# The high part of p on VectorE instead of ScalarE in the loop's last steps

## The chip, the cores and the metric

The kernel runs on one core of a Trainium2 chip. The metric is device time in microseconds (us). A core has five engines, each with its own queue of instructions in a fixed order: TensorE (PE, matrix products), VectorE (DVE), ScalarE (ACT), GpSimd (POOL) and SyncE (SP, which here issues all DMAs). An engine starts an instruction when it is at the head of its queue and its semaphores have come.

## The reference

```python
def _A_ref(x, wqkv, wo):                 # H = 32 heads of 20, window W = 256
    q, k, v = ...                        # x @ wqkv
    scores = einsum("bhqd,bhkd->bhqk", q, k) * Dh ** -0.5
    mask = (idx[:, None] - idx[None, :] >= 0) & (idx[:, None] - idx[None, :] < W)
    p = softmax(where(mask, scores, -1e9))
    o = einsum("bhqk,bhkd->bhqd", p, v)
    return o... @ wo
def _B_ref(x, w1, b1, w2, b2):
    r = relu(x @ w1 + b1)
    return (r * r) @ w2 + b2

xn = layernorm(x)                        # x: 1 x 2048 x 640, f32
return x + _A_ref(xn) * silu(_B_ref(xn))
```

## The kernel before

Products are made in f16 with each operand split in a high and a low part (high = the value rounded to f16, low = the rest), so that a product is three matmuls: high x high, high x low, low x high. The same holds for the softmax weights p: `ph` is p in f16, `pl` is p - ph in f16, and both are multiplied with the values (which have their own two parts in one tile).

After a first stage (layernorm, transposes, values, first queries and keys) a loop of 269 steps runs over 16 pairs of heads (`NP`) times 16 blocks of 128 rows (`NT`), 256 blocks in all, as a software pipeline. In step s:

- the scores of block s (`scores`, L585) and their row maxima (`maxima`, L596, VectorE), as long as s < 256
- `scores_t` (L634, TensorE): the transposed scores of block s-10, into the one PSUM tile `stps`
- `exps` of block s-10: the exponential on ScalarE (L639, from stps into one of three `p32` tiles, `p` in the profile), then two masks on GpSimd (L640, L642)
- `low` of block s-12 (L653, VectorE): pl = p32 - ph. It is the last reader of that p32 tile
- a first share of filler work on TensorE (queries and keys, MLP, output products), then evacuations of filler results (`flush`: `ysb` L936, `sq` L909 on VectorE) and one piece of weight preparation (`tick`: in these steps wo, L1004 high part and L1005 low part, both VectorE)
- `high` of block s-11 (L647): ph from p32
- the rest of the filler share
- in every second step `values` (L667, TensorE) of blocks s-14 and s-13, which read ph and pl; every fourth block ends a group, followed by `normed` (ACT L674 `osb`, DVE L678 `rs`, POOL L680 and L683) and `halves_high`/`halves_low` (ACT L694, DVE L698 `onp`), whose results go to DRAM

All engines run in the order in which the program calls them (`manual_schedule`); there is no scheduler. `state[2]` holds the step number. The steps from 256 to 268 have no scores and no maxima; they finish blocks 246 to 255. Their row maxima still go from a copy `mrow` (L617) by DMA into `qs`, which scores_t reads. Tiles in rotation: three of p32, six of ph, five of pl, one of stps.

Behind the loop the output products (`wops`, L731) run on TensorE, with L1023 and L1024 on VectorE and a Silu on ScalarE (L1038).

Of the kernel before, what the change touches and what calls it, by code (L numbers as in the profile page):

```python
# [11 lines left out]
AF = mybir.ActivationFunctionType  # L12
# [8 lines left out]
NT = S // P  # L21
KC = D // P
NP = H // 2
# [35 lines left out]
def attn_mlp_kernel(ctx: ExitStack, tc, x, wqkv, wo, w1, b1, w2, b2, out):  # L59
    nc = tc.nc  # L60
# [583 lines left out]

    def high(p, kb, p32, n):
        ph = at4.tile([P, 2, 3 * P], F16, tag="ph", name="ph")
        nc.scalar.activation(ph[:, :, :n], p32[:, :, :n], AF.Copy)  # L647
        phs[p, kb] = (ph, p32, n)

    def low(p, kb):  # L650
# [52 lines left out]
    state = [0.0, 0.0, 0]  # L703
# [378 lines left out]
    with tc.manual_schedule(engines={E_.PE, E_.Activation, E_.DVE, E_.Pool, E_.SP}):  # L1082
# [5 lines left out]
        for s in range(steps):  # L1088
# [51 lines left out]
            if c:  # L1140
                high(*c, *exs.pop(c))
# [44 lines left out]
```

## Time and profile before

| | us |
|---|---|
| median of 3 runs | 814.17 (813.47 to 814.29) |
| the profiled execution | 814.96 |
| its span, first to last instruction | 813.2 |
| steps from the first without scores to the last pl | about 715.5 to 742.2 |
| first and last `ph` of the eleven that the change moves | 717.68, 740.04 |

A row of the timeline gives start and duration in us, engine, line, operation, what it writes and reads, and in brackets how long the engine had been idle before it and what it waited for. A row of a window gives busy time of PE, weight loads, DVE, ACT and POOL in that stretch, each with a count of instructions. In rows grouped by line stand busy time, the mean in ns, and idle time before it with its cause.

### The profile page before, as it was taken

What the parts mean: (1) busy time and instruction counts of PE and PEld (TensorE: products, weight loads), DVE (VectorE), ACT (ScalarE), POOL (GpSimd) and SP (SyncE); (2) the same over time, 40 slices, a digit from 0 to 9 for tenths busy, and PEclk for the clock granted to TensorE, in tenths of its full rate; (3) what the DMA queues carried; (4) which work ended last, traced back from release to release, by engine and by line L of the source; (5) the groups of instructions that cost most, each with busy time, mean ns of one, the idle gap of its engine ahead of it and who ended that gap; (6) DMA issues with size and microseconds to landing.
All of it is one profiled execution on the core that took longest, in us unless ns stands there. A gap on an engine that the chain in (4) does not pass through costs nothing.

```text
span 813.2 us, 25075 instructions
## 1 busy us (share of the span) xinstructions
PE 802.0 (99%) x9358; PEld 536.3 (66%) x9358; DVE 698.0 (86%) x1948; ACT 644.6 (79%) x1059; POOL 498.8 (61%) x874
## 2 busy tenths in 40 slices
PE   8999999999999999999999999999999999999998
PEld 7775563455555567777777777777777767767776
DVE  6777666798999999999999999999999999996554
ACT  5466454999899999899999999999989989987200
POOL 2000001467677789897988889888978988783000
PEclk9999999999999999999999999999999999999999
DMA  7995757774665532221222222222221362156994
GB/s 246 256 337 154 195 162 230 241 200 113 160 178 141 158 93 69 58 71 35 69 67 39 68 72 55 55 68 52 51 71 36 86 220 59 14 141 162 281 285 143
DMA packets 157137, 105.49 MB, mean 130 GB/s; under 512 B 101080, under 2 KB 131544, under 8 KB 157016
## 3 DMA queue, kind: packets, MB, share of 16 engines
q1 hardware_dynamic: 157016, 103.90, 46.3%
q8 instruction: 73, 1.20, 0.6%
q14 instruction: 48, 0.39, 0.2%
HBM read 60.43 MB, written 36.83 MB: 120 GB/s over the span
## 4 chain that ended last, share of the span: by engine, by line
PE 82%; ACT 6%; DVE 5%; DMA 3%; issue 3%; SPq 0%; DVEq 0%; ACTq 0%
PE hps L731 20%; PE yps L932 18%; PE wops L731 8%; PE ops L667 8%; PE qkps L731 7%; PE sps L585 7%; PE vps L303 6%; PE stps L634 4%; PE qkps L529 3%; ACT p L639 2%; DVE pl L653 1%; DMA raw<-in_B_w_dram 1%; DMA wvr<-in_A_wqkv_dram 1%; DVE junk L596 1%; DMA raw<-in_A_wqkv_dram 1%
## 5 line engine op out<-in xcount | busy, mean ns | idle before, releaser
L639 ACT ACTIVATE p<-stps,ebias,esc 128x768 f32<-128x768 f32 (+2 forms) x256 | 242.1, 946 | 36.4 <-PE stps L634 15.9
L653 DVE TENSOR_TENSOR pl<-p,ph 128x768 f16<-128x768 f32 (+2 forms) x256 | 250.9, 980 | 0.9 <-PE ops L667 0.8
L596 DVE CUSTOM_DVE_ANT_0 junk<-sps,mask 128x320 bf16<-128x320 f32 (+2 forms) x512 | 220.1, 466 | 27.2 <-PE sps L585 23.6
L640 POOL TENSOR_SCALAR_AFFINE_SELECT p<-p 128x256 f32<-128x256 f32 x256 | 176.3, 689 | 63.9 <-ACT p L639 61.7
L647 ACT ACTIVATE ph<-p 128x768 f16<-128x768 f32 (+2 forms) x256 | 203.0, 793 | 1.0 <-POOL p L640 0.8
L731 PE MATMUL hps<-xT,w 128*128 128x256 f16 x1440 | 190.0, 273 | 0.0
L932 PE MATMUL yps<-w,hh 128*128 128x320 f16 x1152 | 186.7, 300 | 0.0
L731 PEld LDWEIGHTS <-w 128*128 128x128 f16 x1440 | 132.4, 98 | 45.0 <-issue 25.5
L932 PEld LDWEIGHTS <-hh 128*128 128x128 f16 x1152 | 105.0, 98 | 54.9 <-issue 20.9
L731 PE MATMUL qkps<-xT,qkw 128*128 128x512 f16 x480 | 115.5, 380 | 0.0
L642 POOL TENSOR_SCALAR_AFFINE_SELECT p<-p 128x256 f32<-128x256 f32 x224 | 107.6, 480 | 0.0
L667 PE MATMUL ops<-vp,ph 128*128 128x41 f16 x1440 | 89.8, 181 | 0.0
L667 PE MATMUL ops<-vp,pl 128*128 128x41 f16 x1440 | 89.5, 180 | 0.0
L667 PEld LDWEIGHTS <-ph 128*128 128x128 f16 x1440 | 84.6, 96 | 5.2
L585 PE MATMUL sps<-ks,qs 60*64 60x320 f16 (+2 forms) x1024 | 84.5, 313 | 3.2 <-DVE mt L596 2.7
L667 PEld LDWEIGHTS <-pl 128*128 128x128 f16 x1440 | 78.9, 96 | 5.1
L634 PE MATMUL stps<-qs,ks 62*64 62x320 f16 (+4 forms) x1024 | 78.5, 290 | 1.3 <-ACT p L639 0.9
L910 POOL TENSOR_TENSOR hh<-sq,hh 128x256 f16<-128x256 f32 x96 | 66.5, 693 | 21.0 <-DVE sq L909 13.8
L603 POOL CAST mp<-mt 128x8 f16<-128x8 f32 x64 | 45.1, 705 | 54.2 <-DVE mt L596 53.8
L731 PEld LDWEIGHTS <-qkw 128*128 128x128 f16 x480 | 42.5, 98 | 53.5 <-issue 11.0
L303 PE MATMUL vps<-wv,xT 128*128 128x320 f16 x480 | 69.6, 299 | 1.3 <-DVE xT L277 0.4
L731 PE MATMUL wops<-wo,oT 128*128 128x320 f16 (+1 forms) x495 | 65.6, 295 | 0.0
(153 smaller groups left out, 993.3 us busy)
## 6 DMA issues: line engine op xcount, KB each, us to landing
raw<-in_B_w_dram SPq DMA_DIRECT2D x24, 320.0 KB
ks<-k_d SPq DMA_DIRECT2D x64, 120.0 KB
qs<-q_d SPq DMA_DIRECT2D x64, 120.0 KB
v_d<-vt SPq DMA_DIRECT2D x8, 656.0 KB
vp<-v_d SPq DMA_DIRECT2D x16, 328.0 KB
xt<-in_A_x_dram SPq DMA_DIRECT2D x16, 320.0 KB
k_d<-shm SPq DMA_DIRECT2D x20, 256.0 KB
q_d<-shm SPq DMA_DIRECT2D x20, 256.0 KB
```

The costliest lines, as they stand in the source:

```text
L303: nc.tensor.matmul(ps, xT[b][:, xp, c, t * P:(t + 1) * P], wv[wp][:, c, nh * HALF:(nh + 1) * HALF], start=n == 0, stop=n == 3 * KC - 1)
L585: nc.tensor.matmul(ps[HB * j:HB * (j + 1), :nk], qs[i][rows_, q0:q0 + HB], ks[i][rows_, k0:k0 + nk], start=True, stop=True)
L596: nc.vector.tensor_tensor_reduce(out=junk[:, :nk], in0=ps[:, :nk], in1=mk, scale=1.0 / MAX_UNIT, scalar=-3.0e38, op0=ALU.add, op1=ALU.max, ...
L634: nc.tensor.matmul(ps[HB * j:HB * (j + 1), hh, c0:c1], ks[i][rows_, kb * P + HB * j:kb * P + HB * (j + 1)], qs[i][rows_, kb * P + c0:kb * ...
L639: nc.scalar.activation(p32[:, :, :n], ps[:, :, :n], AF.Exp, scale=esc[0], bias=ebias)
L640: nc.gpsimd.affine_select(p32[:, :, 0:P], p32[:, :, 0:P], pattern=[[0, 2], [1, P]], compare_op=ALU.is_ge, fill=0.0, base=0, channel_multip ...
L642: nc.gpsimd.affine_select(p32[:, :, 2 * P:], p32[:, :, 2 * P:], pattern=[[0, 2], [-1, P]], compare_op=ALU.is_gt, fill=0.0, base=0, channel ...
L647: nc.scalar.activation(ph[:, :, :n], p32[:, :, :n], AF.Copy)
L653: nc.vector.tensor_sub(pl[:, :, :n], p32[:, :, :n], ph[:, :, :n])
L667: nc.tensor.matmul(ot[:, q % 4, hh, :], t[:, hh, (q - k) * P:(q - k + 1) * P], vp[:, k // 4, k % 4, hh, :], start=m == 1, stop=m == 2 * le ...
L731: nc.tensor.matmul(ps, a, b_, start=j == 0, stop=j == n - 1)
L932: nc.tensor.matmul(ps, hh[:, hp, tt * P:(tt + 1) * P], lin1(w2t, (2 * fc + wp) * D + nh * HALF, HALF), start=fc == 0 and j == 0, stop=fc = ...
```

## The change

In steps 256 and later, `high` makes ph on VectorE instead of ScalarE. Nothing else is edited; lines below it move down by three.

```diff
     def high(p, kb, p32, n):
         ph = at4.tile([P, 2, 3 * P], F16, tag="ph", name="ph")
-        nc.scalar.activation(ph[:, :, :n], p32[:, :, :n], AF.Copy)
+        if state[2] < NP * NT:
+            nc.scalar.activation(ph[:, :, :n], p32[:, :, :n], AF.Copy)
+        else:
+            nc.vector.tensor_copy(ph[:, :, :n], p32[:, :, :n])
         phs[p, kb] = (ph, p32, n)
```

Step 256 converts block 245 and step 266 block 255, so eleven conversions change engine. In the rows that follow, `p_15267` is the p32 tile of block 245, `p_15296` that of 246, then `p_15364`, `p_15400`, `p_15451`, `p_15484` (block 250), `p_15541` and `p_15575` (block 252).

VectorE's queue at steps 256 to 258, before:

```order
L909 TENSOR_TENSOR sq<-relu 128x256
L617 COPY mrow<-mtp 16x128
L678 RECIPROCAL rs<-osb 128x8
L653 TENSOR_TENSOR pl<-p_15267,ph 128x768
L936 SCALAR_TENSOR_TENSOR ysb<-yps,w_i,b2t 128x320
L1004 TENSOR_SCALAR wo_13868<-raw,wo_s 128x640
L1005 SCALAR_TENSOR_TENSOR wo_13868<-raw,wo_s,wo_13868 128x640
L653 TENSOR_TENSOR pl<-p_15296,ph 128x768
```

and with the change:

```order
L912 TENSOR_TENSOR sq<-relu 128x256
L650 CAST ph<-p_15267 128x768
L617 COPY mrow<-mtp 16x128
L681 RECIPROCAL rs<-osb 128x8
L656 TENSOR_TENSOR pl<-p_15267,ph 128x768
L939 SCALAR_TENSOR_TENSOR ysb<-yps,w_i,b2t 128x320
L1007 TENSOR_SCALAR wo_13868<-raw,wo_s 128x640
L1008 SCALAR_TENSOR_TENSOR wo_13868<-raw,wo_s,wo_13868 128x640
L650 CAST ph<-p_15296 128x768
L656 TENSOR_TENSOR pl<-p_15296,ph 128x768
```

The first conversion stands ahead of mrow and rs, the second directly ahead of the pl that reads it.

The same queue at steps 260 to 264, where the wo pieces end, before:

```order
L678 RECIPROCAL rs<-osb 128x8
L653 TENSOR_TENSOR pl<-p_15451,ph 128x768
L1004 TENSOR_SCALAR wo_13869<-raw,wo_s 128x640
L1005 SCALAR_TENSOR_TENSOR wo_13869<-raw,wo_s,wo_13869 128x640
L653 TENSOR_TENSOR pl<-p_15484,ph 128x768
L936 SCALAR_TENSOR_TENSOR ysb<-yps,w_i,b2t 128x320
L653 TENSOR_TENSOR pl<-p_15541,ph 128x768
L698 TENSOR_TENSOR onp<-on,onp 128x160
L653 TENSOR_TENSOR pl<-p_15575,ph 128x768
```

and with the change:

```order
L650 CAST ph<-p_15451 128x768
L681 RECIPROCAL rs<-osb 128x8
L656 TENSOR_TENSOR pl<-p_15451,ph 128x768
L1007 TENSOR_SCALAR wo_13869<-raw,wo_s 128x640
L1008 SCALAR_TENSOR_TENSOR wo_13869<-raw,wo_s,wo_13869 128x640
L650 CAST ph<-p_15484 128x768
L656 TENSOR_TENSOR pl<-p_15484,ph 128x768
L939 SCALAR_TENSOR_TENSOR ysb<-yps,w_i,b2t 128x320
L650 CAST ph<-p_15541 128x768
L656 TENSOR_TENSOR pl<-p_15541,ph 128x768
L650 CAST ph<-p_15575 128x768
L701 TENSOR_TENSOR onp<-on,onp 128x160
```

Each step gains one conversion behind its evacuation or wo piece; it waits for GpSimd's masks of its block, and the pl behind it waits for it instead of for ScalarE.

ScalarE's queue at steps 256 to 258, before:

```order
L907 ACTIVATE hh<-relu 128x256
L647 ACTIVATE ph<-p_15267 128x768
L674 ACTIVATE osb<-ops 128x328
L639 ACTIVATE p_15364<-stps,ebias,esc 128x768
L647 ACTIVATE ph<-p_15296 128x768
L639 ACTIVATE p_15400<-stps,ebias,esc 128x768
```

and with the change:

```order
L910 ACTIVATE hh<-relu 128x256
L677 ACTIVATE osb<-ops 128x328
L639 ACTIVATE p_15364<-stps,ebias,esc 128x768
L639 ACTIVATE p_15400<-stps,ebias,esc 128x768
L639 ACTIVATE p_15451<-stps,ebias,esc 128x768
```

The conversions are gone from it, so osb and the exponentials follow each other directly. The queues of TensorE, GpSimd and SyncE keep their instructions and their order.

## The prediction

> **What bounds the kernel now.** First the page's busy times and the windows by stage.
>
> ```profile
> span 813.2 us, 25075 instructions
> PE 802.0 (99%) x9358; PEld 536.3 (66%) x9358; DVE 698.0 (86%) x1948; ACT 644.6 (79%) x1059; POOL 498.8 (61%) x874
> 719.00:736.00 17.00, 16.26 (x187) 11.07 (x186) 16.48 (x23) 12.30 (x16) 13.36 (x19) 1.00 0.82 210
> 736.00:746.00 10.00, 10.00 (x137) 7.70 (x135) 5.04 (x9) 6.50 (x11) 3.13 (x5) 1.00 0.74 206
> 745.96 63.90 PE L731 MATMUL wops<-wo,oT 128*128 128x320 f16 x484
> ```
>
> (The window rows give length, then busy time of PE, weight loads, DVE, ACT and POOL, the granted clock and the DMA.) Over the whole span TensorE is the bound: 802.0 of 813.2 us. The change only touches the steps behind the last scores, so the row that decides is that of 719 to 736 us. There VectorE (DVE) is the full engine, 16.48 of 17.00 us, and ScalarE (ACT) has 4.70 us free. TensorE loses 0.74 us. Behind it, from 745.96 us, TensorE runs the output products without a hole to the end: what it loses ahead of them is added to the span in full.
>
> Next, who waits for whom between 719 and 740 us, and the rows behind it (start, duration, and in brackets the wait that came before):
>
> ```profile
> ACT p L639 <- DVE pl L653: 3.4, 4, 1.2
> PE stps L634 <- ACT p L639: 0.5, 2, 0.4
> 734.43 0.99 ACT L639 ACTIVATE p<-stps,ebias,esc 128x768 f32<-128x768 f32 x1 [0.93 <-DVE pl L653]
> 736.28 0.77 ACT L639 ACTIVATE p<-stps,ebias,esc 128x512 f32<-128x512 f32 x1
> 725.28 0.50 PE L634 MATMUL stps<-qs,ks 62*64 62x320 f16 x4 [0.20 <-DMA qs<-mrow]
> 732.81 0.33 PE L634 MATMUL stps<-qs,ks 62*64 62x320 f16 x4 [0.37 <-ACT p L639]
> 735.47 0.30 PE L634 MATMUL stps<-qs,ks 62*64 62x256 f16 x4 [0.18 <-ACT p L639]
> 737.76 0.24 PE L634 MATMUL stps<-qs,ks 62*64 62x128 f16 x4
> ```
>
> This is a ring over three engines. The exponentials of key block k write a p32 tile; there are three, so they need the one that pl of block k-3 has read. TensorE's next stps needs the one stps bank, which those exponentials read. So a late pl on VectorE delays an exponential, and that delays TensorE's queue. At 735.47 us TensorE waits 0.18 us for the exponential that began at 734.43 us, which had waited 0.93 us for pl: the ring is closed here, with no slack left. One step on, the exponential of 736.28 us ends at 737.05, 0.71 us ahead of the stps at 737.76: slack is back.
>
> **The change part by part.** Eleven conversions leave ScalarE and enter VectorE: steps 256 to 266 convert key blocks 245 to 255. Nine are 128x768, the last two 128x512 and 128x256. ScalarE is freed of 0.83 us a step, but it waits in these steps anyway. VectorE gets the conversion behind the evacuations and the wo piece of the step, right ahead of the next pl, which then waits for it. Here is VectorE's queue at the place:
>
> ```profile
> 717.48 0.62 DVE L909 TENSOR_TENSOR sq<-relu 128x256 f32<-128x256 f32 x1
> 718.02 0.20 DVE L617 COPY mrow<-mtp 16x128 f16<-16x128 f16 x1
> 718.87 0.20 DVE L678 RECIPROCAL rs<-osb 128x8 f32<-128x8 f32 x1 [0.64 <-ACT osb L674]
> 718.99 0.91 DVE L653 TENSOR_TENSOR pl<-p,ph 128x768 f16<-128x768 f32 x1
> 720.28 0.72 DVE L1004 TENSOR_SCALAR wo<-raw,wo_s 128x640 f16<-128x640 f32 x1
> 721.03 0.90 DVE L1005 SCALAR_TENSOR_TENSOR wo<-raw,wo_s,wo 128x640 f16<-128x640 f32 x1
> 721.86 1.21 DVE L653 TENSOR_TENSOR pl<-p,ph 128x768 f16<-128x768 f32 x1
> 729.12 0.54 DVE L1004 TENSOR_SCALAR wo<-raw,wo_s 128x640 f16<-128x640 f32 x1
> 733.18 1.15 DVE L653 TENSOR_TENSOR pl<-p,ph 128x768 f16<-128x768 f32 x1
> 734.72 0.94 DVE L653 TENSOR_TENSOR pl<-p,ph 128x768 f16<-128x768 f32 x1
> ```
>
> *The price c of one conversion.* The trace of before has none on VectorE. Nearest is wo's high part, also f32 to f16 from SBUF, one input tensor, 640 elements a row.
>
> ```profile
> L1004 DVE TENSOR_SCALAR wo<-raw,wo_s x5: 537/689/721, 720.3 to 731.6; 128x640 f16<-128x640 f32 x5
> L246 DVE TENSOR_SCALAR xn<-xt,mv,rstd x16: 611/612/614, 5.6 to 81.6; 128x640 f32<-128x640 f32 x16
> L653 DVE TENSOR_TENSOR pl<-p,ph 128x768 f16<-128x768 f32 x224 | 232.6, 1038 | 0.1
> 728.42 0.71 POOL L680 TENSOR_TENSOR on<-osb 128x160 f32<-128x160 f32 x1 [0.49 <-ACT osb L674]
> 729.92 0.93 POOL L640 TENSOR_SCALAR_AFFINE_SELECT p<-p 128x256 f32<-128x256 f32 x1 [0.79 <-ACT p L639]
> 724.84 1.12 POOL L642 TENSOR_SCALAR_AFFINE_SELECT p<-p 128x256 f32<-128x256 f32 x1
> 725.61 0.69 DVE L1004 TENSOR_SCALAR wo<-raw,wo_s 128x640 f16<-128x640 f32 x1
> ```
>
> The fast one of the five (0.54 us, at 729.12) fell almost wholly into a hole of GpSimd (729.13 to 729.92 us); the one at 725.61 us began under a select and took 0.69. A second per-partition operand costs about 0.07 us (0.61 of xn against 0.54), so with none the 640 elements take an estimated 0.47 us. 128 more elements add 0.11 us at that row's rate (0.54/640 each): 0.58 us free of GpSimd, and 0.15 more beside a select, 0.73. I take **c = 0.65 us**, between them, since GpSimd is busy 13.36 of 17.00 us but with holes. The ends: 0.50 (640 elements in 0.54 us, less the operand, with nothing for length) and 1.04 us, the mean of a pl, if the conversion runs like an operation of two tensors. Below nothing it can't go: it is work added to an engine that is full.
>
> The Trainium skill, "VectorE: DVE Perf Modes", section "The perf-mode tier table", gives 1227 ns for an f32 copy of 2048 elements in SBUF, twice as fast as a two-tensor operation; scaled by its rate of two elements a cycle, the estimate is 0.56 us for 768 elements, and the sum below would be 2.5 us by it.
>
> *What lies beside other work.* The first conversion, block 245, comes between sq and mrow at 718.02 us. VectorE idles 0.64 us right there, waiting for osb, and osb on ScalarE stood behind a conversion that is gone:
>
> ```profile
> 717.68 0.83 ACT L647 ACTIVATE ph<-p 128x768 f16<-128x768 f32 x1
> 718.41 0.42 ACT L674 ACTIVATE osb<-ops 128x328 f32<-128x328 f32 x1
> 717.71 0.18 PE L667 MATMUL ops<-vp,pl 128*128 128x41 f16 x1
> 717.63 0.50 SPq L1013 DMA_DIRECT2D xres<-in_A_x_dram  x1
> 718.25 1.39 SPq L711 DMA_DIRECT2D qs<-mrow  x2
> xres<-in_A_x_dram SPq DMA_DIRECT2D x1, 1280.0 KB
> ```
>
> With the values done at about 717.89 us, osb can end at 718.4 instead of 718.83. Then 718.02 + 0.65, mrow, rs (each starting some 0.08 us ahead of the end before it) let pl of block 245 begin at 718.82 instead of 718.99: c - 0.82 = -0.17 us. For this one the cover is complete; without it, it would cost c more, 0.65 us. mrow goes out about 0.6 us later on SP's queue; its landing, which TensorE waited for at 725.28 us (0.20 us), came seven microseconds after the copy, behind the load of xres (1280 KB in one issue) ahead of it on that queue. So I cost it at nothing; uncovered, it would cost TensorE 0.6 us at that place, not in addition, since the ring delays the later stps by more.
>
> *What lies on the path.* Between pl of block 245 and pl of block 250 (733.18 us) VectorE gets five conversions in a full queue. Three stand right ahead of their pl, which must wait for the result: c + 0.03 each (wo's low part begins 0.03 us behind the high part: 720.28 + 0.72 to 721.03). Two have onp or rs between, where the next starts some 0.08 us before the end: c - 0.08 each. Sum: -0.17 + 3 x 0.68 + 2 x 0.57 = **3.0 us** (6c - 0.9 in general). So pl of block 250 ends at 737.3 instead of 734.33 us, its exponential starts at 737.4 and ends at 738.4, and stps of step 264 starts 3.0 us later, at 738.5 instead of 735.47. ScalarE does not bind here: one exponential of 0.99 us a step is left to it.
>
> Behind that the wo pieces are over. pl of block 251 ends 3.7 us later, at 739.4 (735.66 before, plus c + 0.03), the exponential of block 254 at 740.2, and TensorE reaches its stps at 737.76 + 3.0 = 740.8: 0.6 us to spare. The values of the last blocks have their pl over 1 us ahead in the same way. So six of the eleven conversions set the loss, and the other five cost nothing; without the slack each would cost c, 0.65 us. The stalls of 0.37 and 0.18 us that TensorE has now lie inside the 3.0, since it is counted from stps' own start.
>
> A rule that speaks against the change stands in the Trainium skill, "SBUF — State Buffer", section "Who interferes with whom": a conversion on VectorE in a two-port mode and a GpSimd instruction exclude each other for the whole instruction. By that rule a conversion beside a select would wait it out, 0.40 us (its shortest here) or more. The rows bear out only a part: 0.15 to 0.18 us more for wo's high part, and 1.12 instead of 0.40 us for the select.
>
> **The rivals.** (1) *Dearer conversions.* Each waits for a whole select, by the row below 0.40 us at its shortest: c = 0.58 + 0.40 = 0.98, sum 5.0 us; or it runs at pl's 1.04, sum 5.3 us. That gives span 818.2 to 818.5, and on the median 819.2 to 819.5. (The first is the rule of the Trainium skill's page "SBUF — State Buffer", named above.) For it: selects grew to 1.12 us. Against: wo's high part never passed 0.72.
>
> ```profile
> 720.25 0.40 POOL L640 TENSOR_SCALAR_AFFINE_SELECT p<-p 128x256 f32<-128x256 f32 x1
> ```
>
> (2) *The collisions only move.* The selects start about 1.2 us behind pl's end, and now the conversion stands where pl stood. Then pl falls from 1.15 to the 0.94 of 734.72 us, 0.2 us in each of five, and the sum with c = 0.50 to 0.58 is 2.1 to 2.6 less 1.0, so 1.1 to 1.6 us: 815.3 to 815.8 on the median. For it: 0.91 to 1.21 us of one and the same pl. Against: the two selects of a block cover more than one conversion.
>
> (3) *Not slower.* If pl's wait for ScalarE were what holds VectorE, or if the recorded wait for pl really were another one, the exponentials would start earlier with ScalarE freed of 0.83 us, and TensorE would win back its 0.55 us for them: 813.6 on the median. The place is stps of steps 263 and 264. By the sum it decides below c = 0.15 us (6c = 0.9). Against: the four exponentials that wait for pl start right behind its end (734.33 to 734.43), VectorE's rows show no wait for ph there, and no operation of this width is near 0.15 us.
>
> (4) *It doesn't do what it says.* Eleven tiles move, not ten, but the eleventh is one of those with slack: no difference.
>
> **How the numbers follow.** The profiled execution took 814.96 us, 1.76 around the span of 813.2, and is 0.8 above the median of 814.17. Forecast: span 816.2, that execution 818.0, the median **817.2 us**. Chances: forecast (1.6 to 4.3 us) 0.64; rival 1 0.14; rival 2 (up to 1.6) 0.16; rival 3 0.06. Leaving out most of rival 3, the small end of rival 2 and what lies beyond 5.2 us gives 814.9 to 819.4. A measurement of this kernel tells some 0.2% from no change, 1.6 us. Slower by more than that (forecast and rival 1): 0.78; within it (rival 2 and most of rival 3): 0.20; faster: 0.02.
>
> **What would show it.** Conversions of 0.58 to 0.73 us on VectorE; pl of block 250 ending near 737.3; VectorE still full until then; longer waits of the exponentials for pl; TensorE's holes between 725 and 739 us growing from 0.75 to some 3.7 us; the run of output products unchanged in length, 3 us later. A conversion near 1 us, or a hole behind step 264, would show rival 1 or a missed wait; exponentials that no longer follow a pl, rival 3.

## The result, and the profile after

The change makes the kernel slower: median 818.84 us of 6 runs against 814.05 us of 6 runs of the kernel before, ratio 1.0057, 95% interval 1.0047 to 1.0068 (+3.8 to +5.5 us). Measured twice more, it gave 1.0049 (1.0035 to 1.0062) and 1.0045 (1.0033 to 1.0057).

Page and windows of the changed kernel, in the columns of before; the stretch is shifted by 0.47 us, since that much lay ahead of it already (below):

```profile
span 817.3 us, 25077 instructions
PE 802.8 (98%) x9358; PEld 537.0 (66%) x9358; DVE 704.9 (86%) x1959; ACT 637.4 (78%) x1048; POOL 498.6 (61%) x874
719.47:736.47 17.00, 13.81 (x166) 9.61 (x165) 16.69 (x24) 5.76 (x8) 11.19 (x16) 1.00 0.74 187
750.00 63.90 PE L734 MATMUL wops<-wo,oT 128*128 128x320 f16 x484
```

Over the whole span almost nothing is to be seen: VectorE is 6.9 us busier, ScalarE 7.2 us less. In the stretch TensorE fell from 16.26 to 13.81 us busy, with VectorE as full as it was (16.69 of 17.00) and ScalarE down from 12.30 to 5.76. The run of output products is as long as before and starts at 750.00 instead of 745.96 us.

The waits, from 719.5 to 744 us, and TensorE's scores_t rows with the exponentials ahead of two of them:

```profile
ACT p L639 <- DVE pl L656: 12.9, 7, 2.6
PE stps L634 <- ACT p L639: 3.7, 4, 1.4
728.87 0.33 PE L634 MATMUL stps<-qs,ks 62*64 62x320 f16 x4 [0.76 <-ACT p L639]
732.58 0.33 PE L634 MATMUL stps<-qs,ks 62*64 62x320 f16 x4 [1.37 <-ACT p L639]
736.17 0.33 PE L634 MATMUL stps<-qs,ks 62*64 62x320 f16 x4 [0.75 <-ACT p L639]
739.51 0.30 PE L634 MATMUL stps<-qs,ks 62*64 62x256 f16 x4 [0.86 <-ACT p L639]
741.80 0.24 PE L634 MATMUL stps<-qs,ks 62*64 62x128 f16 x4
738.47 0.99 ACT L639 ACTIVATE p<-stps,ebias,esc 128x768 f32<-128x768 f32 x1 [2.34 <-DVE pl L656]
740.46 0.78 ACT L639 ACTIVATE p<-stps,ebias,esc 128x512 f32<-128x512 f32 x1 [0.78 <-DVE pl L656]
```

The exponentials wait 12.9 instead of 3.4 us for pl, TensorE 3.7 instead of 0.5 us for the exponentials. The last such wait is that of step 264 (739.51). The stps of step 265 (741.80) has none, though the exponential that must leave the stps bank for it (740.46 + 0.78 = 741.24) waited too: 0.56 us to spare. mrow's DMA, a wait of 0.20 us before, is gone from TensorE's rows.

VectorE's queue: the six conversions that count with their pl, and one conversion behind them:

```profile
717.95 0.62 DVE L912 TENSOR_TENSOR sq<-relu 128x256 f32<-128x256 f32 x1
718.49 0.76 DVE L650 CAST ph<-p 128x768 f16<-128x768 f32 x1
719.17 0.20 DVE L617 COPY mrow<-mtp 16x128 f16<-16x128 f16 x1
719.41 1.18 DVE L656 TENSOR_TENSOR pl<-p,ph 128x768 f16<-128x768 f32 x1
722.55 0.81 DVE L650 CAST ph<-p 128x768 f16<-128x768 f32 x1
723.39 1.04 DVE L656 TENSOR_TENSOR pl<-p,ph 128x768 f16<-128x768 f32 x1
725.88 0.76 DVE L650 CAST ph<-p 128x768 f16<-128x768 f32 x1
726.75 0.97 DVE L656 TENSOR_TENSOR pl<-p,ph 128x768 f16<-128x768 f32 x1
729.01 0.76 DVE L650 CAST ph<-p 128x768 f16<-128x768 f32 x1
730.14 1.28 DVE L656 TENSOR_TENSOR pl<-p,ph 128x768 f16<-128x768 f32 x1
733.18 0.76 DVE L650 CAST ph<-p 128x768 f16<-128x768 f32 x1
734.05 0.97 DVE L656 TENSOR_TENSOR pl<-p,ph 128x768 f16<-128x768 f32 x1
736.52 0.76 DVE L650 CAST ph<-p 128x768 f16<-128x768 f32 x1
737.38 0.97 DVE L656 TENSOR_TENSOR pl<-p,ph 128x768 f16<-128x768 f32 x1
738.73 0.54 DVE L650 CAST ph<-p 128x768 f16<-128x768 f32 x1
L650 DVE CAST ph<-p 128x768 f16<-128x768 f32 x9 | 6.8, 756 | 0.0
```

A conversion costs 0.76 us (mean of nine 0.756). The one at 738.73 us took 0.54. GpSimd's rows say why:

```profile
736.19 0.67 POOL L640 TENSOR_SCALAR_AFFINE_SELECT p<-p 128x256 f32<-128x256 f32 x1 [0.87 <-ACT p L639]
736.82 0.72 POOL L642 TENSOR_SCALAR_AFFINE_SELECT p<-p 128x256 f32<-128x256 f32 x1
739.52 1.08 POOL L640 TENSOR_SCALAR_AFFINE_SELECT p<-p 128x256 f32<-128x256 f32 x1 [1.98 <-ACT p L639]
```

The conversion at 738.73 us lies wholly in GpSimd's hole from 737.54 to 739.52 us. The one at 736.52 us began while the first select ran, which ended at 736.86 us, and itself ended at 737.28, 0.42 us behind it.

This holds throughout. The ten profiles with conversions in these steps, those of the change and of the experiments, hold 83 conversions of 128x768 on VectorE. Of these, 69 began while a GpSimd instruction was running and ended 0.40 to 0.43 us behind its end, whether 0.22 or 0.48 us of it were left. The other 14 found none running at their start and took 0.54 or 0.55 us. We read this as a wait: a conversion sits out the rest of the GpSimd instruction that runs as it starts.

**A ruler for the experiments.** From the start of sq in step 256 to the start of the closed run of output products: 745.96 - 717.48 = 28.48 us before, 750.00 - 717.95 = 32.05 us with the change, so **3.57 us** belong to these steps. Where sq starts scatters from run to run, whatever the kernel; this stretch repeats within 0.03 us for each of the three programs profiled more than once, as the following shows.

### The profile page after: what moved, and what is told of

The parts are those of the page before. It is cut to its first block, busy times and chain, and to the rows that moved or that the text cites. A ratio compares the mean times of both kernels' runs of the same rounds, so it can differ in the third digit from the quotient of the medians.

```text
span 817.3 us, 25077 instructions
## 1 busy us (share of the span) xinstructions
PE 802.8 (98%) x9358; PEld 537.0 (66%) x9358; DVE 704.9 (86%) x1959; ACT 637.4 (78%) x1048; POOL 498.6 (61%) x874
## 4 chain that ended last, share of the span: by engine, by line
PE 81%; ACT 6%; DVE 6%; issue 3%; DMA 3%; POOL 1%; SPq 0%; DVEq 0%; ACTq 0%
PE hps L734 19%; PE yps L935 18%; PE wops L734 8%; PE ops L670 8%; PE qkps L734 7%; PE sps L585 7%; PE vps L303 6%; PE stps L634 4%; PE qkps L529 3%; ACT p L639 2%; DVE pl L656 1%; DMA wvr<-in_A_wqkv_dram 1%; ACT ph L648 1%; DMA raw<-in_A_wqkv_dram 1%; DVE junk L596 1%
## 5 line engine op out<-in xcount | busy, mean ns | idle before, releaser
L648 ACT ACTIVATE ph<-p 128x768 f16<-128x768 f32 x245 | 194.5, 794 | 0.2
```

## The experiments

| run | what is on VectorE | sq to products, us | against 28.48 | ratio to before (95%) |
|---|---|---|---|---|
| before_again | as before | 28.47 | -0.01 | 1.0004 (0.9993 to 1.0015) |
| change_again | all eleven | 32.07 | +3.59 | 1.0049 (1.0035 to 1.0062) |
| change_third | all eleven | 32.04 | +3.56 | 1.0045 (1.0033 to 1.0057) |
| early_blocks | blocks 245 to 250 | 32.02 | +3.54 | 1.0042 (1.0028 to 1.0056) |
| early_again | the same | 32.02 | +3.54 | 1.0044 (1.0030 to 1.0058) |
| late_blocks | blocks 251 to 255 | 28.48 | 0.00 | 0.9999 (0.9990 to 1.0008) |
| twice | all, five of them twice | 35.03 | +6.55 | 1.0076 (1.0064 to 1.0088) |
| wo_high_act | as before, less five of wo | 27.55 | -0.93 | 0.9985 (0.9973 to 0.9996) |
| after_wo_high_act | all, less five of wo | 28.70 | +0.22 | 1.0003 (0.9995 to 1.0012) |
| after_p32x4 | all; four p32 tiles | 31.69 | +3.21 | 1.0035 (1.0023 to 1.0046) |
| after_pace2 | all; wo every second step | 29.10 | +0.62 | 1.0003 (0.9994 to 1.0012) |

The edits are made on the changed kernel where nothing else is said.

### Which conversions count

late_blocks:

```diff
-        if state[2] < NP * NT:
+        if state[2] < NP * NT + 6:
```

> Only the conversions of blocks 251 to 255 (steps 262 to 266) are on VectorE; those of 245 to 250 stay on ScalarE. Ring theory (VectorE is full up to pl of block 250, slack behind it): no loss, between -0.3 and +0.5 us against the kernel before, and TensorE's holes around stps of steps 262 to 264 as before (0.2 to 0.6 us). Rival, each conversion counts alike: 5 of 11 of the 4.8 us, about +2.2 us. Rival, the extra over the trace's 3.6 us has to do with the edit as such and not with its place: +0.5 to +1.2 us.

early_blocks and early_again:

```diff
-        if state[2] < NP * NT:
+        if not NP * NT <= state[2] < NP * NT + 6:
```

> Only the conversions of blocks 245 to 250 (steps 256 to 261) are on VectorE. Ring theory: the whole loss of the change, 6c - 0.9 with c = 0.76 measured, so +3.6 us in the profile, up to +4.8 us by the medians. Rival, each conversion counts alike: 6 of 11, about +2.6 us.

> The conversions of blocks 245 to 250 alone on VectorE, again, beside the two others on the same chip. Ring theory: the same loss behind step 256 as the change, 3.5 to 3.6 us in the profile; by the medians +3.0 to +4.2 us. If it stays below the change by 1 us, that lies ahead of step 256, not in the conversions of blocks 251 to 255.

The waits of late_blocks from 712 to 745 us:

```profile
ACT p L639 <- DVE pl L656: 6.3, 7, 1.7
PE stps L634 <- ACT p L639: 0.9, 3, 0.5
737.09 0.24 PE L634 MATMUL stps<-qs,ks 62*64 62x128 f16 x4
```

Five conversions behind pl of block 250 cost nothing, 0.00 us, though exponentials wait 6.3 us for pl: those waits end ahead of TensorE, whose stps of step 265 (737.09) has no wait. The first six bring the whole 3.54 of 3.57 us. "Each conversion counts alike" (2.2 and 2.6 us) falls. The holes of 0.9 us are also those of the kernel before in another run: before_again had 0.21, 0.52 and 0.18 us at the stps of steps 262 to 264, where the first profile had 0.37 and 0.18 and the DMA's 0.20.

### More of the same cost

twice, behind the conversion:

```diff
             nc.vector.tensor_copy(ph[:, :, :n], p32[:, :, :n])
+            if 1 <= state[2] - NP * NT < 6:
+                nc.vector.tensor_copy(ph[:, :, :n], p32[:, :, :n])
```

> The change, and in steps 257 to 261 each conversion of VectorE is made a second time onto the same tile. Ring theory: five more conversions ahead of pl of block 250, each 0.76 to 0.85 us with its wait: +3.8 to +4.3 us on top of the change, so +8 to +9 us against the kernel before by the medians. Rival, another wait takes over (the ring is no longer the longest path): less than +2 us on top of the change.

Measured: 2.98 us more than the change in the stretch, below the 3.8 to 4.3 expected and above the rival's 2. By the medians it is 6.7 us above the kernel before, where 8 to 9 was expected. One such pair in twice, and the select beside it:

```profile
736.59 0.76 DVE L650 CAST ph<-p 128x768 f16<-128x768 f32 x1
737.39 0.64 DVE L652 CAST ph<-p 128x768 f16<-128x768 f32 x1
738.13 0.96 DVE L658 TENSOR_TENSOR pl<-p,ph 128x768 f16<-128x768 f32 x1
736.90 0.72 POOL L642 TENSOR_SCALAR_AFFINE_SELECT p<-p 128x256 f32<-128x256 f32 x1
740.25 0.30 PE L634 MATMUL stps<-qs,ks 62*64 62x256 f16 x4 [1.53 <-ACT p L639]
```

The second one took 0.64 us instead of the 0.76 that the expectation used: 0.23 us of the select were left at its start (to 737.62), and it ended 0.41 us behind that. Five are 3.2 us. The stps of step 264 still waits for the exponential behind pl of block 250. So the path is still VectorE's queue, and the expectation's price was off: too dear here, where the prediction's was too low.

### Taking work off the full engine

wo_high_act, on the kernel before; after_wo_high_act is the same edit on the change:

```diff
-                nc.vector.tensor_scalar(hi, raw, mlp["so"], None, ALU.mult)
+                nc.scalar.activation(hi, raw, AF.Copy, scale=mlp["so"])
```

> The kernel before, with the high part of wo made by ScalarE instead of VectorE in steps 257 to 261 (five instructions of 0.69 us leave the full engine). Ring theory: the exponentials stop waiting for pl, and TensorE's holes of 0.37 and 0.18 us at stps of steps 263 and 264 go: -0.3 to -0.75 us. Rival, ScalarE's place in the ring matters as well (0.7 to 0.8 us more in its queue each step, and the low part waits for it): 0 to +2 us.

> The change, and wo's high part made by ScalarE in steps 257 to 261: five instructions of 0.54 to 0.74 us leave VectorE, which the conversions of 0.76 us entered. Theory of a full VectorE: the loss goes almost wholly, -0.6 to +0.8 us against the kernel before; sq to output products 28.0 to 29.3 us. Rival, the loss comes from the conversions holding up GpSimd and its masks: it stays at +3 us or more.

wo_high_act beats both kernels: 812.65 us median of 12 runs, ratio 0.9985. The 0.93 us in the stretch are about what TensorE lost at its stps (0.91 us in before_again), and more than the 0.3 to 0.75 us expected, which left out a part of that loss. The stps of step 264 has no wait left, and ScalarE's rows show a step with no idle time, at no price to TensorE:

```profile
719.45 0.99 ACT L639 ACTIVATE p<-stps,ebias,esc 128x768 f32<-128x768 f32 x1
720.33 0.83 ACT L1004 ACTIVATE wo<-raw,wo_s 128x640 f16<-128x640 f32 x1
721.05 0.84 ACT L647 ACTIVATE ph<-p 128x768 f16<-128x768 f32 x1
721.78 0.99 ACT L639 ACTIVATE p<-stps,ebias,esc 128x768 f32<-128x768 f32 x1
732.93 0.30 PE L634 MATMUL stps<-qs,ks 62*64 62x256 f16 x4
```

On the change, the same edit takes 3.35 of the 3.57 us back. What counts is VectorE's load: once something of about equal size leaves, the same conversions beside the same masks cost 0.22 us against the kernel before. They aren't free: against wo_high_act itself, 27.55 us, they cost 1.15. The rival (GpSimd and its masks held up), which had 3 us or more staying, falls.

after_pace2 keeps all work on VectorE and only spreads it:

```diff
-        return 2 if kind == "s" and state[2] > 2 * LAG else 1
+        return 2 if kind == "o" or kind == "s" and state[2] > 2 * LAG else 1
```

> The change with the five wo pieces in every second step (257, 259, 261, 263, 265) instead of in five steps running. Theory of a full VectorE: two steps then cost it some 5.3 us against 4.9 us of TensorE instead of 6.6: the loss falls to +0.3 to +2.0 us. Rival, the loss is set by the number of conversions: it stays at +3.6 us.

With the same eleven conversions, 0.62 us are left in the stretch. So most of the loss is the meeting of the conversions with the five wo pieces. What this pacing alone gives the kernel before wasn't run, so the 0.62 us is no price of the conversions by themselves.

### The ring, or the queue behind it

after_p32x4:

```diff
-        p32 = at2.tile([P, 2, 3 * P], F32, tag="p32", bufs=3, name="p32")
+        p32 = at2.tile([P, 2, 3 * P], F32, tag="p32", bufs=4, name="p32")
```

> The change with four p32 tiles instead of three: the exponential of block k then waits for pl of block k-4. If the ring over the three tiles were all that ties TensorE to VectorE, the loss would go: 0 to +0.5 us. If VectorE's full queue is the cause and the ring only the first place at which TensorE meets it, the values of step 262 wait for pl of block 249 instead (2.9 us later than before): +2.5 to +3.2 us, sq to output products 31.0 to 31.7 us, with the wait at L670.

TensorE's rows that waited in it, in step 262:

```profile
728.77 0.33 PE L634 MATMUL stps<-qs,ks 62*64 62x320 f16 x4
732.42 0.19 PE L670 MATMUL ops<-vp,ph 128*128 128x41 f16 x1 [1.46 <-DVE ph L650]
733.48 0.22 PE L670 MATMUL ops<-vp,pl 128*128 128x41 f16 x1 [0.87 <-DVE pl L656]
```

The exponentials no longer hold up stps, and the values of step 262 wait for the conversion and then pl of block 249, as expected. But these waits are 2.33 us together, where TensorE waited 4.01 us for VectorE in the change (3.74 at stps, 0.27 at the values of step 262). Against the 0.75 us of before they explain 1.58 of the 3.21 us. Most of the rest lies in the step that follows. Here are its filler matmuls before and in this run, and a window of this run, with the granted clock behind the five busy times (0.50):

```profile
733.08 2.21 PE L932 MATMUL yps<-w,hh 128*128 128x320 f16 x15
734.25 3.40 PE L935 MATMUL yps<-w,hh 128*128 128x320 f16 x15
733.40:736.70 3.30, 3.22 (x21) 1.86 (x22) 3.16 (x5) 1.22 (x2) 3.03 (x5) 0.50 1.13 201
```

Right behind the waits, from 733.4 to 736.7 us, TensorE's granted clock was 0.50, and fifteen matmuls took 3.40 instead of 2.21 us. From stps of step 263 to that of step 264 went 3.75 us instead of 2.48 (2.66 less its wait of 0.18), 1.27 us more; the remaining 0.36 of the 3.21 us isn't split up. The windows of before and of the change show a granted clock of 1.00 here. The executions fit, though the start of sq scatters by as much: the two with a granted clock of 1.000 over the span took 815.41 and 815.80 us, the four with 0.998 took 816.58 to 817.51.

So the ring over three tiles was a part of the price, and the values behind it the next place where TensorE meets VectorE's lateness. That the 31.69 us came out at the upper end of the expected 31.0 to 31.7 was luck: the wait was smaller, and a fall of the clock that no sum held made up for it.

### What scatters

> The kernel before, word for word, run like the others: what the measurement makes of no change. Between -0.7 and +0.7 us. In its profile 28.4 to 28.6 us from sq of step 256 to the closed run of output products; sq itself anywhere from 715.5 to 718 us if the start of the kernel is what scatters.

> The change once more, beside other runs of the kernel before. From the start of sq in step 256 to the start of the closed run of output products the profile had 28.48 us before and 32.05 us with the change, 3.57 us more; sq itself started at 715.6 to 718.0 us in the profiles so far, whatever the kernel. Ring theory, with the rest of the 4.8 us from that spread ahead of the change: 32.0 to 32.1 us again, and +3.0 to +4.3 us by the medians. Rival, the edit costs something ahead of step 256 as well: +4.5 us or more by the medians.

> The change a third time. If the 0.9 to 1.2 us by which its medians (+4.8, +4.5 us) stood above the profile's 3.6 us were scatter: +3.0 to +4.2 us. If this program really loses some 1 us ahead of step 256: +4.3 to +5.2 us again, with sq at 717 us or later in its profile.

In the profiles of before and before_again, the same kernel, sq of step 256 started at 717.48 and 715.11 us (spans 813.2 and 810.9), and from sq on they differ by 0.01 us. With the change sq started at 717.95, 717.29 and 716.00 us. So the start scatters by over 2 us, and 715.11 lies below the 715.5 that was expected. The medians of the change stood 4.8, 4.5 and 3.9 us above before. The 4.5 of change_again missed the expected 3.0 to 4.3 and reached the bound of its rival, a cost ahead of step 256; the 3.9 of change_third, with sq at 716.00 us, speaks against that rival. The intervals of the second and third take in 3.57 us (ratio 1.0044), the first (from 1.0047) does not. That these 0.3 to 1.2 us are scatter is likely, with early_blocks, twice and the others within 0.5 us of their profiles, but it isn't shown.

A run with the conversions and without GpSimd's masks wasn't made: that GpSimd lengthens the conversions rests on the rows above.

## Why the prediction was right

The direction and the mechanism hold, the size was low: +3.0 us forecast, +3.57 in the stretch, +3.9 to +4.8 by the medians. The first median's +4.8 lies above the 4.3 us up to which the forecast's own chance reached, and inside the stated range only through the room left for rival 1, whose price was not the reason. What lies between 3.57 and 4.8 us stood in no term of the sum, and that the range took it in was luck.

- **The place.** "TensorE's next stps": the shift is set at stps of step 264, 739.51 - 717.95 = 21.56 us from sq instead of 17.99, which is the 3.57 us; none is added behind it. Shown by late_blocks (0.00) and early_blocks (3.54). Of the slack behind it 0.56 us was left, where the prediction had 0.6. TensorE's waits were to grow from 0.75 to some 3.7 us, and were 4.01.
- **The first conversion.** It went into the hole as said. pl of block 245 came 1.46 instead of 1.51 us behind sq, -0.05 us; the term said -0.17, the conversion being dearer by 0.11.
- **The five on the path: the mis-sized term.** 3.18 us was said, from pl of block 245 to that of 250; measured 17.97 - 14.19 = 3.78 us. The price c = 0.65 was between a free one and one beside a select, 0.58 and 0.73, "since GpSimd is busy 13.36 of 17.00 us but with holes". Both ends were near (0.54 and 0.76), but all five began while a GpSimd instruction was running (0.81, then 0.76 four times), so the holes counted for nothing. With their mean, 0.77, the term's own form, 5c - 0.07, gives the 3.78. The other work between them cancels nearly: pl of blocks 245 to 249 took 5.44 us together, 5.46 before. The selects start a little over 1 us behind pl's end, by way of the exponential, and that is where the conversion now stands: rival 2 had said so.
- **Rival 2, the collisions only move.** Half right in its mechanism, and not in its sum: pl of blocks 246 to 250 took 5.23 instead of 5.70 us together, 0.47 less, not 1.0; the conversions took 0.2 us more each; and pl of block 245 took 1.18 instead of 0.91, which the rival left out. What is won is the 0.18 in pl of block 250 itself: -0.05 + 3.78 - 0.18 = 3.55, 0.02 off the shift measured.
- **Rival 1, a whole select waited out.** Not so: 0.22 us more beside GpSimd (0.76 against 0.54), not 0.40 or more. But that "the rows bear out only a part" of exclusion was a misreading, already in the trace of before. The four slow high parts of wo (0.69 to 0.72 us) each ended 0.34 or 0.35 us behind the end of the GpSimd instruction that ran as they began: the one at 725.61 us ended at 726.30, the select of 724.84 at 725.96. So each followed the rest of that instruction, 0.34 to 0.37 us, though only 0.15 to 0.18 us of it shows beside the 0.54 of the free one. The Trainium skill's rule of mutual exclusion for the whole instruction ("SBUF — State Buffer", "Who interferes with whom") agrees with this and with the 69 conversions above (0.40 to 0.43 us behind GpSimd's end). The 5.0 us came from letting a conversion wait for a whole select on top of its own time; the measurement decides against that size.
- **Rival 3, not slower.** ScalarE freed of work won nothing: its waits for pl grew to 12.9 us. wo_high_act shows the reverse: more work on ScalarE, less on VectorE, 0.93 us won.
- **mrow.** Costed at nothing, and stps of step 260 had no wait for its DMA. The one wait not foreseen: the values of step 262 waited 0.3 us for pl in the change. The next stps waited for its exponential in any case, so this cost nothing of its own.

## What to carry to other kernels

Read the load of an engine in the stretch where the change acts, not over the span: VectorE at 86% of the span was 97% full in the 17 us that decided. Work moved onto a full engine cost its length for each instruction that met no hole, up to the last place where another engine had no slack, and nothing behind that place. One more buffer moved the wait to the next consumer and shortened it, from 4.01 to 2.33 us. A time that hardly moves doesn't show that the cause stayed: compare the waits and the granted clock first. If work has to move there, move something of equal size away, or spread what it meets.

## What was not expected of the hardware

A conversion 128x768 from f32 to f16 on VectorE takes 0.54 or 0.55 us when no GpSimd instruction runs at its start (14 of 83), and otherwise ends 0.40 to 0.43 us behind the end of that instruction. That makes 0.64 us where 0.23 us of it were left, 0.76 where 0.34 or 0.35 were, and 0.88 where 0.47 were. In these steps pl ranges from 0.91 to 1.28 us. Against ScalarE's 0.83 us for the same tile VectorE is the faster engine for it, and the kernel is still slower with it there.

In after_p32x4 TensorE's granted clock fell to 0.50 for at least 3.3 us, right behind waits of 1.46 and 0.87 us with one matmul between them. In twice, with a wait of 1.84 us at 731.99 us, it was 1.00 from 729.5 to 735 us. What makes the difference isn't shown.
